# RWKV-7 recurrence and a cosine-gated MLP on one core: first loads in another order, back substitution over more segments, k, v, r behind x^T, sine passes and weight pieces in smaller works

## The chip, the core and the metric

The kernel runs on one core of a Trainium2 chip. A core has five engines with an instruction stream each: PE (TensorE, matrix products; its weight loads are listed as PEld), DVE (VectorE), ACT (ScalarE), POOL (GpSimd) and SP (SyncE, here only an issuer of DMAs). Each stream is worked off in order, and an engine waits on semaphores for the others. The metric is the device time of one execution in microseconds, the median of several runs.

## The reference

Two blocks follow each other. The first is a recurrence with a 40 x 40 state for each of 4 batches and 8 heads over 768 tokens, the second an MLP on its output, turned into 3072 tokens of 320 channels, with 2048 hidden units and g = h cos(h). The weights come as 64-bit floats.

```python
for t in range(S):
    y[:, :, t] = np.einsum('bhd,bhde->bhe', rt, state)
    Sa = np.einsum('bhde,bhe->bhd', state, at)
    state_decay = state * wt[:, :, None, :] - np.einsum('bhd,bhe->bhde', Sa, bt)
    state = state_decay + np.einsum('bhd,bhe->bhde', vt, kt)
...
h = x @ w_in
g = h * np.cos(h)
return g @ w_out
```

## The kernel before

**Chunks.** The recurrence runs over 24 chunks of 32 tokens (`NCH`, variable `c`), the four batches together on 128 partitions. A chunk is written as a list of *segments*, each a group of matmuls on PE and the work that takes their results out of PSUM:

- `t`, `q`, `x`, `s`, `z` (`ch_t` to `ch_z`, tiles `sT`, `qps`, `x0ps`, `sps`, `dps`) are the chain of the chunk itself. `z` renews the state `qz` and makes the output `yt`; the next `t` reads `qz`, so two chunks follow each other strictly.
- `v`, `k`, `g` (`p2_v`, `p2_k`, `p2_g`, tiles `vT`, `kT`, `gram`) prepare the next chunk from k, v and r.
- `p1` prepares chunks two at a time, some chunks ahead, from w, a and b: `p1_w` (tile `wT`; scans into `wb`, L311), `p1_a` twice (tile `wn`; reciprocal L327 and product `aT` L329), `p1_b` (tile `bT`) and `p1_n` (tile `nps`, product `nt`). Below these are w, a, a', b and n. In the main loop they are the list `extra`.

**Back substitution.** For every four chunks DVE inverts triangular 32 x 32 systems: `inv_start` transposes `nt` into `u` (L373), 31 times `inv_step` multiplies and subtracts (L381, L385; sizes rise from 31 to 256 elements per partition and fall again), `inv_end` transposes the result into `rt` (L389), which `s` of the four chunks reads. These 33 works stand in the list `inv_steps`, and the main loop puts some of them behind each step.

**Weights.** Each of 36 weight pieces comes as 64-bit words by a DMA from POOL's queue (`fetch`, three buffers `words`) and is turned into single precision in three works, `exponent`, `mantissa`, `product` (L197 to L219), on DVE and ACT. They stand in `w_steps`.

**The MLP** runs over 12 groups of two chunks (`g`) and four slices of the hidden units (`j`), in *pieces*: `first_a` and `first_b` (tile `ph`), then twice `second` (tile `po`) for the slice before. `first_b` also emits the sine passes: ACT adds a rounding constant (L614), DVE takes the fraction of the turns (L616), ACT takes the absolute value and the sine (L618, L619), DVE multiplies (L623). The products also free the PSUM of `ph`.

**x^T.** `tokens` sends `yt` to DRAM (`xd`) and, one step later, back as `xT`, both by SP's queue. The loads of k, v, r and w, a, b go by the same queue.

**The order** is written out by hand: `step` emits a work, then what `later` has put off by so many steps, then works of `inv_steps` and `w_steps`. The main loop emits the segments of a chunk, and after each the pieces that are due: eight per chunk, by a lag `START` of 2.4 chunks. So which engine does what in which order is fixed at build time, and an instruction waits for everything ahead of it on its engine. PSUM has two buffers (`at`) for all segments, two (`ps_h`) for `ph`, two (`ps_o`) for `po`.

## Time and profile before

| | us |
|---|---|
| median of 3 runs | 976.82 |
| lowest, highest | 975.35, 978.05 |
| the profiled execution | 975.64 |
| its span in the trace | 973.6 |
| PE, DVE, ACT, POOL busy | 782.4, 535.9, 355.3, 185.9 |

The profile page slices the span into 40 equal parts; each digit is a busy share in tenths, PEclk the clock that TensorE was granted. It shows a start of some ten slices in which DVE is full and PE is not, then a stretch in which PE is nearly full but for a dip about every sixth slice, and an end that PE fills alone.

```profile
PE   3605546686998997998888999888899887999987
DVE  4498887689426279335479324587335573233222
PEclk9555556787999997999997999999999998999999
```

The rows of the views that carry numbers stand in the prediction.

### The profile page before, as it was taken

To read this page: it belongs to the slowest core of one execution; us is meant where nothing else is said; L and a number is where in the kernel's file an instruction comes from. 1 tells how busy PE (TensorE), PEld (TensorE's weight loads), DVE (VectorE), ACT (ScalarE), POOL (GpSimd) and SP (SyncE) were. 2 spreads that over 40 slices of the span, in tenths; PEclk is the share of its full clock that TensorE was granted. 3 is DMA by queue.
4 is the path that set the end of the run, shared out by engine and by line. 5 is a ranking of instruction groups with operands and counts; after the bars stand their busy time and mean duration, and the time that the engine had idled before them with its cause. 6 is when DMAs were issued, how large, how long until landed. Compare 5 with 4: busy or idle time off the path is not lost.

```text
span 973.6 us, 36928 instructions
## 1 busy us (share of the span) xinstructions
PE 782.4 (80%) x16472; PEld 602.9 (62%) x16472; DVE 535.9 (55%) x1178; ACT 355.3 (36%) x671; POOL 185.9 (19%) x372
## 2 busy tenths in 40 slices
PE   3605546686998997998888999888899887999987
PEld 2504445465776675777666677666677665777765
DVE  4498887689426279335479324587335573233222
ACT  0103525441352432443432433422434332444333
POOL 4303342202123012023102112102202202111000
PEclk9555556787999997999997999999999998999999
DMA  6512637221321311312212213213211201200000
GB/s 95 94 29 84 155 87 157 63 52 20 70 42 38 57 37 30 65 38 48 50 35 45 48 38 55 56 22 55 45 32 37 51 3 36 44 25 17 23 23 13
DMA packets 181470, 49.06 MB, mean 50 GB/s; under 512 B 159040, under 2 KB 179008, under 8 KB 181312
## 3 DMA queue, kind: packets, MB, share of 16 engines
q1 hardware_dynamic: 174016, 35.56, 19.7%
q0 software_dynamic: 2944, 10.49, 3.6%
q8 instruction: 129, 2.11, 0.9%
q10 hardware_dynamic: 4352, 0.66, 0.4%
q14 instruction: 29, 0.24, 0.1%
HBM read 38.80 MB, written 7.86 MB: 48 GB/s over the span
## 4 chain that ended last, share of the span: by engine, by line
PE 49%; DVE 23%; ACT 10%; issue 6%; SPq 5%; DMA 4%; POOL 2%; POOLq 0%; ACTq 0%; DVEq 0%
PE ph L101 21%; PE po L101 13%; SPq L149 5%; DVE inv_tmp L381 4%; DVE inv L385 4%; ACT turns L614 2%; DVE wb L311 2%; PE qps L101 2%; PE gram L101 2%; DVE turns L616 2%; ACT turns L619 2%; ACT turns L618 2%; DMA xT<-xd 2%; PE sT L464 2%; PE dps L101 2%
## 5 line engine op out<-in xcount | busy, mean ns | idle before, releaser
L101 PE MATMUL po<-w_out_sb,gT 128*128 128x320 f32 x768 | 237.1, 455 | 1.0 <-issue 1.0
L101 PE MATMUL ph<-xT,w_in_sb 128*128 128x256 f32 x768 | 203.3, 412 | 22.6 <-DMA xT<-xd 14.3
L616 DVE SCALAR_TENSOR_TENSOR turns<-turns,ph 128x512 f32<-128x512 f32 x96 | 61.7, 684 | 259.3 <-ACT turns L614 259.3
L101 PEld LDWEIGHTS ph<-xT,w_in_sb 128*128 128x128 f32 x768 | 149.6, 204 | 48.3 <-issue 24.1
L101 PEld LDWEIGHTS po<-w_out_sb,gT 128*128 128x128 f32 x768 | 144.1, 197 | 56.7 <-issue 9.2
L614 ACT ACTIVATE turns<-ph,rnd 128x512 f32<-128x512 f32 x96 | 60.8, 684 | 150.3 <-PE ph L101 150.3
L554 POOL TENSOR_TENSOR qz<-qz,wc 128x160 f32<-128x160 f32 x92 | 41.4, 466 | 332.2 <-DVE qz L553 331.6
L623 DVE TENSOR_TENSOR gT<-ph,turns 128x512 f32<-128x512 f32 x96 | 63.1, 684 | 23.6 <-ACT turns L619 23.6
L385 DVE TENSOR_TENSOR inv<-inv,inv_tmp 128x31 f32<-128x31 f32 (+15 forms) x186 | 68.6, 369 | 6.4
L381 DVE TENSOR_TENSOR inv_tmp<-u,inv 128x31 f32<-128x31 f32 (+15 forms) x186 | 68.3, 367 | 5.1
L619 ACT ACTIVATE turns<-turns,half_pi 128x512 f32<-128x512 f32 x96 | 69.3, 722 | 3.1
L618 ACT ACTIVATE turns<-turns 128x512 f32<-128x512 f32 x96 | 59.7, 622 | 10.4 <-DVE turns L616 10.4
L101 PE MATMUL ph<-xT,w_in_tail 64*128 64x256 f32 x384 | 55.1, 406 | 0.0
L327 DVE RECIPROCAL rw<-wn 128x320 f32<-128x320 f32 x24 | 51.5, 2145 | 2.1 <-PE wn L270 2.1
L468 ACT COPY s<-sT 128x512 f32<-128x512 f32 x46 | 24.7, 588 | 58.5 <-PE sT L464 58.5
L200 ACT ACTIVATE expo<-expo,to_bits 128x256 int32<-128x256 int32 (+1 forms) x36 | 19.2, 533 | 72.7 <-DVE expo L197 72.7
L101 PEld LDWEIGHTS ph<-xT,w_in_tail 64*128 64x128 f32 x384 | 33.5, 188 | 18.8 <-issue 15.8
L522 ACT COPY sm<-sps 128x160 f32<-128x160 f32 x48 | 14.0, 291 | 77.8 <-DVE sm L526 43.4
L270 PE MATMUL wT<-ident,nat_w 128*128 128x128 f32 x88 | 14.6, 315 | 34.2 <-DVE x L505 23.7
L313 POOL COPY wc<-wb 128x16 f32<-128x16 f32 x24 | 5.4, 225 | 186.0 <-DVE wb L311 186.0
L101 PE MATMUL dps<-vvm,kn 32*64 32x72 f32 x1536 | 27.3, 255 | 16.8 <-ACT vvm L456 8.4
L101 PE MATMUL gram<-aT,kT 40*32 40x32 f32 x1536 | 19.2, 211 | 26.8 <-DVE wb L311 23.1
(104 smaller groups left out, 1107.7 us busy)
## 6 DMA issues: line engine op xcount, KB each, us to landing
words<-in_moe_w_out_dram POOLq DMA_DIRECT2D x16, 320.0 KB, 3.7
words<-in_moe_w_in_dram POOLq DMA_DIRECT2D x16, 256.0 KB, 3.6
nat_k<-in_k_dram SPq DMA_DIRECT2D x96, 40.0 KB
nat_v<-in_v_dram SPq DMA_DIRECT2D x96, 40.0 KB
nat_r<-in_r_dram SPq DMA_DIRECT2D x96, 40.0 KB
xd<-yt SPq DMA_DIRECT2D x48, 80.0 KB
out_dram<-ot SPq DMA_DIRECT2D x24, 160.0 KB
nat_w<-in_w_dram SPq DMA_DIRECT2D x88, 40.0 KB
```

Source lines behind the costliest of these rows:

```text
L101: nc.tensor.matmul(o, lhsT=lhsT, rhs=rhs, start=start, stop=stop, skip_group_check=True)
L149: via.dma_start(nat[n, c][blk[i], :, :D], src[n][i, :, c * C : (c + 1) * C, :].rearrange("h t d -> t h d"),)
L327: nc.vector.reciprocal(rw, unpad(ps[:, 0].rearrange("p (h d) -> p h d", h=H)))
L381: nc.vector.tensor_tensor(tmp, u[:, :j, j : j + 1].to_broadcast([P, j, C - j]), x[:, j : j + 1, j:].to_broadcast([P, j, C - j]), ALU.mult,)
L385: nc.vector.tensor_tensor(x[:, :j, j:], x[:, :j, j:], tmp, ALU.subtract)
L468: nc.scalar.copy(G["s"][:, 4 * i : 4 * i + 4].rearrange("p i e -> p (i e)"), ps[:, i])
L554: nc.gpsimd.tensor_tensor(z, z, wc.rearrange("p (f m b) -> p f m b", f=2, m=2)[:, :, :, bb] .unsqueeze(3).to_broadcast([P, 2, 2, D]), ALU. ...
L614: nc.scalar.activation(n, u, ACTF.Identity, bias=rnd, scale=1.0)
L616: nc.vector.scalar_tensor_tensor(n, n, -ROUND, u, ALU.add, ALU.subtract)
L618: nc.scalar.activation(n, n, ACTF.Abs)
L619: nc.scalar.activation(n, n, ACTF.Sin, bias=half_pi, scale=-2.0 * math.pi)
L623: nc.vector.tensor_tensor(gT[:, 2 * e : 2 * e + 2].rearrange("p f t -> p (f t)"), us[e], ns[e], ALU.mult)
```

## The change

It has five parts.

1. **First loads** (`load` calls): w before a, a of chunks 2 and 3 from SP's queue in place of ACT's, then b, w, a, b, k, v, r in the order of first use. The loads of w, a, b for two chunks are interleaved tensor by tensor.
2. **Back substitution**: where a chunk's number leaves 2 on division by four, b and n stand right behind `t` and `q`, and v, k, g behind them; so its works start in that chunk's middle and go on with one per step (before: from the end of that chunk, two per step). Where it leaves 3, w stands behind `t`, and k behind `x`. Works that are left are emitted only ahead of the first `s` that needs `rt`. The buffer `inv` is cleared with the later half of `nt`.
3. **k, v, r** of the next chunk: three separate works, three to five steps after `p2_kn` (before: one work, two steps after), so that SP issues x^T first.
4. **Sine passes**: `first_b` emits absolute value and sine for its first half only; the second half and the products follow one and two steps later, at the latest with the next `first_a`.
5. **Weight pieces**: the mantissa of a piece is emitted between exponent and product of the piece before; `mant` gets a second buffer.

```diff
@@ -151,13 +151,15 @@
                     src[n][i, :, c * C : (c + 1) * C, :].rearrange("h t d -> t h d"),
                 )
 
-    for c in range(4):
+    for c in range(2):
+        load(c, "w")
         load(c, "a", nc.scalar)
-    for c in (0, 2):
-        for n in "wb":
-            load(c, n)
-            load(c + 1, n)
-    load(0, "kvr")
+    for names in ("b", "wab"):
+        for n in names:
+            for c in range(2):
+                load(c if names == "b" else c + 2, n)
+    for n in "kvr":
+        load(0, n)
 
 
 
@@ -201,7 +203,7 @@
 
         def mantissa():
             lo, hi = t["words"][:, :, 0], t["words"][:, :, 1]
-            t["mant"] = sb1.tile([P, DM], I32, tag="mant", name="mant")[:n, :wid]
+            t["mant"] = sb2.tile([P, DM], I32, tag="mant", name="mant")[:n, :wid]
             frac = t["mant"].bitcast(F32)
             nc.vector.tensor_scalar(t["mant"], hi, 0xFFFFF, None, ALU.bitwise_and)
             nc.vector.scalar_tensor_tensor(
@@ -218,7 +220,7 @@
             )
             nc.vector.tensor_tensor(dst, t["mant"].bitcast(F32), expo.bitcast(F32), ALU.mult)
 
-        return fetch, [exponent, mantissa, product]
+        return fetch, exponent, mantissa, product
 
     def weights():
 
@@ -235,7 +237,8 @@
                 for rows, part in src:
                     nc.gpsimd.dma_start(dst[rows], part)
 
-            work.append((fetch, [lambda: nc.scalar.mul(dst, dst, by)]))
+            none = lambda: None
+            work.append((fetch, none, none, lambda: nc.scalar.mul(dst, dst, by)))
 
         for j in range(NF // 4):
             cs = slice(4 * j * P, 4 * (j + 1) * P)
@@ -274,7 +277,7 @@
     flat = lambda t: t.rearrange("p q t -> p (q t)")
     b4 = lambda t: t.rearrange("p (q t) -> p q t", t=C)
     unpad = lambda t: t[:, :, :D]
-    G = {}
+    G = {"rest": []}
 
     waiting = []
 
@@ -362,7 +365,7 @@
                 su.rearrange("p j t -> p (j t)").unsqueeze(1).to_broadcast([P, 2, HH * C]),
                 ALU.mult,
             )
-        if c % 4 == 0:
+        if c % 4 == 2:
             G["inv"] = sb1.tile([P, C * C], F32, tag="inv", name="inv")
             nc.gpsimd.memset(G["inv"], 0.0)
             nc.gpsimd.memset(G["inv"][:, :: C + 1], -1.0)
@@ -409,7 +412,8 @@
         nc.gpsimd.tensor_tensor(unpad(kn_b[c % 2]), nat["k", c], G["rw", c], ALU.mult)
         nc.gpsimd.tensor_copy(vvm[c % 2][:, :, C : C + D], nat["v", c])
         if c + 1 < NCH:
-            later(2, lambda: load(c + 1, "kvr"))
+            for i, n in enumerate("kvr"):
+                later(3 + i if c else 1, lambda n=n: load(c + 1, n))
 
     def p2_v(c):
         ps = at("vT")
@@ -589,7 +593,7 @@
 
 
     def first_a(g, j):
-        products()
+        rest(3)
         G["ph"] = [ps_h.tile([P, 2, 2 * P], F32, tag="h", name="ph") for _ in range(2)]
         G["gT", j] = sb2.tile([P, 4, 2 * P], F32, tag="gT", name="gT")
         first_full(g, j, 0)
@@ -614,22 +618,25 @@
             nc.scalar.activation(n, u, ACTF.Identity, bias=rnd, scale=1.0)
         for u, n in zip(us, ns):
             nc.vector.scalar_tensor_tensor(n, n, -ROUND, u, ALU.add, ALU.subtract)
-        for n in ns:
+        gT = G["gT", j]
+
+        def cosine(n):
             nc.scalar.activation(n, n, ACTF.Abs)
             nc.scalar.activation(n, n, ACTF.Sin, bias=half_pi, scale=-2.0 * math.pi)
-        gT = G["gT", j]
 
         def product(e):
             nc.vector.tensor_tensor(
                 gT[:, 2 * e : 2 * e + 2].rearrange("p f t -> p (f t)"), us[e], ns[e], ALU.mult
             )
 
-        G["products"] = [lambda e=e: product(e) for e in range(2)]
-        later(1, products)
-
-    def products():
-        for work in G.pop("products", ()):
-            work()
+        cosine(ns[0])
+        G["rest"] = [lambda: cosine(ns[1]), lambda: product(0), lambda: product(1)]
+        later(1, lambda: rest(2))
+        later(2, lambda: rest(1))
+
+    def rest(n):
+        for _ in range(min(n, len(G["rest"]))):
+            G["rest"].pop(0)()
 
     def second(g, j, i):
 
@@ -670,8 +677,8 @@
         def last_a():
             p1_a(c + 1)
             if c >= 2 and c + 3 < NCH:
-                for i in range(2):
-                    later(2 + i, lambda i=i: load(c + 2 + i, "wab"))
+                for i in range(6):
+                    later(2 + i, lambda i=i: load(c + 2 + i % 2, "wab"[i // 2]))
 
         return [lambda: p1_w(c), lambda: p1_a(c), last_a, lambda: p1_b(c), lambda: p1_n(c)]
 
@@ -712,8 +719,12 @@
             work()
 
         w_ends = []
-        for n, (_, parts) in enumerate(w_work):
-            w_steps.extend(parts)
+        w_steps.append(w_work[0][2])
+        for n, (_, exponent, _, product) in enumerate(w_work):
+            w_steps.append(exponent)
+            if n + 1 < len(w_work):
+                w_steps.append(w_work[n + 1][2])
+            w_steps.append(product)
             if n + 3 < len(w_work):
                 w_steps.append(w_work[n + 3][0])
             w_ends.append(len(w_steps))
@@ -734,18 +745,21 @@
                 extra = (p1(q0)[3:], p1(q0 + 2)[:3], p1(q0 + 2)[3:])[c % 4]
             if c == 0:
                 segs = [x, v, extra[0], s, k, extra[1], z, g, *extra[2:]]
-            elif len(extra) == 3:
+            elif c % 4 == 1 and extra:
                 segs = [t, v, q, k, x, extra[0], s, g, z, *extra[1:]]
-            elif len(extra) == 2:
+            elif c % 4 == 2 and extra:
+                segs = [t, extra[0], q, extra[1], x, v, s, k, z, g]
+            elif c % 4 == 3 and extra:
+                segs = [t, extra[0], q, v, x, k, s, g, z, *extra[1:]]
+            elif c % 4 == 0 and extra:
                 segs = [t, v, q, k, x, g, s, extra[0], z, extra[1]]
             else:
                 segs = [t, v, q, k, x, g, s, z]
             n = len(segs)
-            if c % 4 == 0:
-                while inv_steps:
+            fill = (1, 4 if c < 2 else 3)
+            for i, seg in enumerate(segs):
+                while seg is s and ("rt", c) not in G:
                     inv_steps.pop(0)()
-            fill = (1 + (c % 4 == 3), 4 if c < 2 else 3)
-            for i, seg in enumerate(segs):
                 step(seg, *fill)
                 due = (c + (i + 1) / n - START) * 8
                 while done < min(due, len(pieces)) and 2 * pieces[done][0] + 2 <= c:
```

The following rows are instructions in the order of their engine's stream: line, operation, result and operands, elements, and how often in a row. The first are DVE's in chunk 7 before, around the scans of `wT` (L311); L381 and L385 are one step of the back substitution.

```order
L505 COPY x_6808<-x0ps 128x288
L623 TENSOR_TENSOR gT<-ph,turns 128x512 x2
L381 TENSOR_TENSOR inv_tmp<-u,inv 128x252
L385 TENSOR_TENSOR inv<-inv,inv_tmp 128x18x14
...
L381 TENSOR_TENSOR inv_tmp<-u,inv 128x255
L385 TENSOR_TENSOR inv<-inv,inv_tmp 128x15x17
L308 MEMSET wT 128x32
L311 SCALAR_TENSOR_TENSOR wb<-wT,w_188 128x512
L311 SCALAR_TENSOR_TENSOR wb<-wT,w_190 128x512
L381 TENSOR_TENSOR inv_tmp<-u,inv 128x252
L385 TENSOR_TENSOR inv<-inv,inv_tmp 128x14x18
```

The same place of the changed kernel, whose lines 311, 314, 384, 388, 620, 628 and 509 are the former 308, 311, 381, 385, 616, 623 and 505:

```order
L384 TENSOR_TENSOR inv_tmp<-u,inv 128x240
L388 TENSOR_TENSOR inv<-inv,inv_tmp 128x20x12
L311 MEMSET wT 128x32
L314 SCALAR_TENSOR_TENSOR wb<-wT,w_188 128x512
L314 SCALAR_TENSOR_TENSOR wb<-wT,w_190 128x512
L384 TENSOR_TENSOR inv_tmp<-u,inv 128x247
L388 TENSOR_TENSOR inv<-inv,inv_tmp 128x19x13
...
L620 SCALAR_TENSOR_TENSOR turns<-turns,ph 128x512 x2
L384 TENSOR_TENSOR inv_tmp<-u,inv 128x255
L388 TENSOR_TENSOR inv<-inv,inv_tmp 128x15x17
L509 COPY x_6831<-x0ps 128x288
L628 TENSOR_TENSOR gT<-ph,turns 128x512
```

Ahead of the scans stand twelve of the 31 steps where there were seventeen, and this chunk's first sine pass (L620) and the copy of `x` (L509) now come behind the scans.

SP's stream at the turn from chunk 19 to 20 before (`xd` and `xT` carry the tokens, the others are loads for a later chunk):

```order
L574 DMA xd<-yt 40x4x128 x2
L149 DMA nat_k<-in_k_dram 32x8x40 x4
L149 DMA nat_v<-in_v_dram 32x8x40 x4
L149 DMA nat_r<-in_r_dram 32x8x40 x4
L584 DMA xT<-xd 128x2x128
L586 DMA xT<-xd 64x128 x2
```

and in the changed kernel:

```order
L578 DMA xd<-yt 40x4x128 x2
L588 DMA xT<-xd 128x2x128
L590 DMA xT<-xd 64x128 x2
L149 DMA nat_k<-in_k_dram 32x8x40 x4
L149 DMA nat_v<-in_v_dram 32x8x40 x4
L149 DMA nat_r<-in_r_dram 32x8x40 x4
```

The twelve loads have moved behind the three DMAs that bring x^T back.

DVE's first weight pieces in chunk 0 before (L197 is the exponent, L206 and L207 the mantissa, L216 and L219 the product):

```order
L197 TENSOR_SCALAR expo<-words 128x256
L206 TENSOR_SCALAR mant<-words 128x256
L207 SCALAR_TENSOR_TENSOR mant<-words,mant 128x256
L216 SCALAR_TENSOR_TENSOR expo<-words,expo 128x256
L219 TENSOR_TENSOR w_in_sb<-mant,expo 128x256
```

and in the changed kernel, where the lines are 199, 208, 209, 218 and 221:

```order
L208 TENSOR_SCALAR mant<-words 128x256
L209 SCALAR_TENSOR_TENSOR mant<-words,mant 128x256
L199 TENSOR_SCALAR expo<-words 128x256
L208 TENSOR_SCALAR mant<-words 128x256
L209 SCALAR_TENSOR_TENSOR mant<-words,mant 128x256
L218 SCALAR_TENSOR_TENSOR expo<-words,expo 128x256
L221 TENSOR_TENSOR w_in_sb<-mant,expo 128x256
```

A mantissa (for the piece after) now stands between a piece's exponent and its product.

## The prediction

> **What bounds the kernel now.** I first read the page's head, then cut the trace at every `sT` group on PE (the first matmuls of a chunk, from chunk 1 on), because the 24 chunks do not have one limit.
>
> ```profile
> span 973.6 us, 36928 instructions
> PE 782.4 (80%) x16472; PEld 602.9 (62%) x16472; DVE 535.9 (55%) x1178; ACT 355.3 (36%) x671; POOL 185.9 (19%) x372
> ```
>
> The table of windows has, per chunk, the length, the busy time of PE, PEld, DVE, ACT and POOL (instructions in brackets), the granted PE clock, the DMA share and GB/s. In order these are chunks 0, 2, 3, 6, 7, 9, 11, 14, 15, 18, 19, 20 and 21.
>
> ```profile
> 75.20:108.40 33.20, 14.15 (x477) 11.65 (x477) 28.50 (x62) 11.75 (x26) 12.71 (x24) 0.50 0.38 99
> 143.70:194.80 51.10, 32.83 (x724) 25.27 (x725) 36.22 (x87) 26.16 (x49) 14.92 (x27) 0.71 0.45 105
> 194.80:244.00 49.20, 35.53 (x637) 27.39 (x636) 44.04 (x108) 16.60 (x32) 7.08 (x14) 0.82 0.17 37
> 311.70:345.90 34.20, 31.71 (x748) 24.00 (x749) 15.56 (x31) 14.12 (x26) 6.17 (x12) 0.95 0.32 61
> 345.90:387.40 41.50, 33.54 (x638) 26.14 (x637) 34.56 (x85) 12.52 (x24) 6.53 (x13) 0.88 0.15 29
> 421.60:453.40 31.80, 30.11 (x637) 23.57 (x636) 12.43 (x25) 12.52 (x24) 6.15 (x13) 1.00 0.18 34
> 487.70:530.10 42.40, 34.84 (x638) 26.81 (x637) 35.10 (x88) 12.52 (x24) 6.64 (x13) 0.84 0.17 32
> 596.00:630.00 34.00, 30.12 (x749) 23.16 (x750) 14.45 (x28) 14.11 (x26) 6.20 (x12) 1.00 0.32 61
> 630.00:671.20 41.20, 32.89 (x637) 25.77 (x636) 35.54 (x88) 12.52 (x24) 6.55 (x13) 0.92 0.17 31
> 737.20:772.20 35.00, 31.74 (x748) 24.00 (x749) 15.92 (x32) 14.11 (x26) 6.25 (x12) 0.95 0.15 34
> 772.20:804.50 32.30, 29.18 (x614) 22.20 (x613) 25.07 (x70) 11.99 (x22) 2.26 (x5) 0.94 0.11 21
> 804.50:841.40 36.90, 30.24 (x614) 22.63 (x613) 13.74 (x33) 12.61 (x24) 5.52 (x11) 0.91 0.16 34
> 841.40:868.90 27.50, 27.34 (x613) 20.84 (x612) 8.90 (x22) 12.43 (x23) 5.39 (x10) 1.00 0.17 33
> ```
>
> Chunk 9 (remainder 1 by four) is PE's: 30.1 us of matmul in 31.8 us, DVE 12.4 us. Chunks 7, 11 and 15 (remainder 3) have the same segments and matmul counts, yet take 41.2 to 42.4 us: DVE is busy for 35 us there, PE's clock falls to 0.84 to 0.92, and PE's own busy time swells to 33 to 35 us. Up to chunk 3, DVE sets the pace too (28.5 of 33.2 us in chunk 0). So the prize is in chunks 3, 7, 11, 15 and 19, and in the start; chunk 21 (27.3 of 27.5 us) shows a chunk in which nothing is left.
>
> PE's timeline in chunk 7 says which waits end last; the bracket is idle time and what ended it:
>
> ```profile
> 360.84 2.32 PE L101 MATMUL po<-w_out_sb,gT 128*128 128x320 f32 x8
> 368.40 0.83 PE L101 MATMUL gram<-aT,kT 40*32 40x32 f32 x60 [4.43 <-DVE wb L311]
> 375.63 0.81 PE L101 MATMUL dps<-vvm,kn 32*64 32x72 f32 x52 [1.95 <-ACT vvm L456]
> 387.35 1.06 PE L464 MATMUL sT<-ident,qz 128*128 128x128 f32 x8 [1.58 <-DVE aT L329]
> ```
>
> All three follow DVE: `gram` needs the PSUM buffer that the scans of `wT` (L311) release. DVE's and POOL's own timelines there:
>
> ```profile
> 345.53 0.21 DVE L385 TENSOR_TENSOR inv<-inv,inv_tmp 128x31 f32<-128x31 f32 x1
> 351.64 0.39 DVE L385 TENSOR_TENSOR inv<-inv,inv_tmp 128x220 f32<-128x220 f32 x1
> 365.91 2.34 DVE L311 TENSOR_TENSOR_SCAN wb<-wT,w 128x512 f32<-128x512 f32 x2
> 380.49 1.20 DVE L381 TENSOR_TENSOR inv_tmp<-u,inv 128x87 f32<-128x87 f32 x1
> 380.29 1.29 POOL L565 TENSOR_TENSOR yt<-yt,wb 128x512 f32<-128x512 f32 x1
> ```
>
> `wT` was on PE by 361.0 us, but its scans start at 365.9 us, behind back-substitution steps.
>
> **The change, part by part.**
>
> *Back substitution.* The page's groups give its price:
>
> ```profile
> L385 DVE TENSOR_TENSOR inv<-inv,inv_tmp 128x31 f32<-128x31 f32 (+15 forms) x186 | 68.6, 369 | 6.4
> L381 DVE TENSOR_TENSOR inv_tmp<-u,inv 128x31 f32<-128x31 f32 (+15 forms) x186 | 68.3, 367 | 5.1
> ```
>
> (68.6 + 68.3) / 6 = 22.8 us for each of the six inversions, plus two transposes; nothing of it is removed. It moves: `b` and `n` go to the front of remainder-2 chunks, so 11 of its 33 works (the transpose and ten steps) issue there, 19 in the remainder-3 chunk, three in the next, one per step. From the rows, the ten small steps take 351.64 + 0.39 - 345.53 + 0.2, about 6.7 us; the last two, short as the first, about 0.9 us. So 15.2 us stay in chunks 7, 11, 15, and DVE has 12.4 + 15.2 = 27.6 us there instead of 35. The segment `w` also moves up, behind `t`; ahead of its scans then stand two steps of this chunk, not the backlog. The wait for the scans becomes that of `v`: between `w` and `v` PE has one piece and `q`, about 3 us, and copies plus scans take 0.3 + 2.34 us and a little queueing: I take 0.7 us. Beside it I leave 1.0 us at `dps` (of 1.95) and 0.4 us at the next `sT`, which needs a 2.1 us reciprocal on a busier DVE than in chunk 9. That gives 31.8 + 0.7 + 1.0 + 0.4 = 33.9, taken as 34 us: bounds are 31.8 (chunk 9) and 41.2 (unchanged). Gain: 41.5 + 42.4 + 41.2 - 3 x 34 = **23.1 us**. Chunk 3 has 44.0 us of DVE work now, 3.5 us of it the last weight pieces and the rest of the inversion; without 7 to 8 us that move out and the stalls, 37.5 us: **11.7 us** (bounds 5 and 15).
>
> The works that arrive in remainder-2 chunks (8.8 us with the transpose) lie beside PE's 30 us: DVE has 15 of 34 us busy. What is late next there is `g`, now right behind `z`, waiting for `z`'s PSUM as `n` did, some 0.7 us longer because a step stands ahead of the adds. With the waits for x^T gone (below) I take 33.5 us: 34.2 + 34.3 + 34.0 - 3 x 33.5 = **2.0 us** (chunk 10 is 34.3 us, between the two shown) and 35.0 - 33.5 = **1.5 us** for chunk 18. If that cover fails, each of these four loses what a remainder-3 chunk loses now (a rival).
> Chunk 19 issues 16 steps instead of 32; 28.3 us, near chunk 21: **4.0 us**.
>
> *x^T before k, v, r on SP's queue.* Chunk 19 to 20, SP first, then PE, and PE at chunk 22, where no such loads are in between:
>
> ```profile
> 806.42 0.70 SPq L574 DMA_DIRECT2D xd<-yt  x2
> 813.07 0.45 SPq L584 DMA_DIRECT2D xT<-xd  x1
> 815.28 2.04 PE L101 MATMUL ph<-xT,w_in_sb 128*128 128x256 f32 x4 [6.60 <-DMA xT<-xd]
> ...
> 874.68 1.97 PE L101 MATMUL ph<-xT,w_in_sb 128*128 128x256 f32 x8 [1.69 <-DMA xT<-xd]
> ```
>
> The 12 loads hold x^T back from 807.1 to 813.1 us; the trip through DRAM still needs xd to land, so I keep 2.0 us of wait as at chunk 22 and 0.3 us of lower clock: 27.5 + 2.3 = 29.8 us, **7.1 us**. In other even chunks this wait was at most 1 us and is in the 33.5. What the loads lose, xd's landing and three issues, some 4 us of lead, hides behind the chunk: in the program their first reader, the copy into `vp`, stands behind this chunk's `g`, and `v` of the chunk after needs it. If that fails, `v` waits.
>
> *First loads.* Rows of ACT, PE and POOL:
>
> ```profile
> 6.20 4.99 ACTq L149 DMA_DIRECT2D w_in_sb<-in_a_dram  x8
> 11.28 1.28 ACT L307 ACT_TABLE_LOAD   x1 [11.28 <-DMA w_in_sb<-in_a_dram]
> 7.89 1.09 PE L270 MATMUL wT<-ident,nat_w 128*128 128x128 f32 x4 [1.74 <-DMA nat_b<-in_b_dram]
> 33.87 0.45 POOL L403 COPY vp<-nat_v 128x320 f32<-128x320 f32 x1
> ```
>
> ACT issues eight loads that nobody needs yet and copies from `wT` at 12.57 us, though PE is done at 9.0 us. Without them the table load falls into the wait for `wT`: 12.57 - 9.1, **3.4 us**. The eight DMAs go to SP, some 5 us of issue, ahead of k, v, r, which then land near 30 us; POOL needs v at 33.87 - 3.4 = 30.5 us, so the cover is thin (if it fails, 1 to 2 us). Bounds 1 and 4.
>
> *Weight pieces.* DVE's waits from 75 to 250 us (total, count, longest) and the page's line of the fetch:
>
> ```profile
> DVE w_in_sb L219 <- ACT mant L210: 7.4, 13, 2.8
> DVE w_out_sb L219 <- ACT mant L210: 4.4, 14, 0.6
> words<-in_moe_w_out_dram POOLq DMA_DIRECT2D x16, 320.0 KB, 3.7
> ```
>
> With the next piece's mantissa ahead of the product, these 11.8 us go. But a piece's words are then needed half a piece earlier, so part may return as a wait for the fetch (3.7 us to land, a piece takes about 3 us with what lies between). I take **5 us** in chunks 0 and 1 and nothing in chunk 2, where DVE gains seven back-substitution us against the rest. Bounds -8 and 12.
>
> *Sine passes.* ACT's second pair (0.62 + 0.72 us) and the products come one or two steps later; the PSUM that they free is needed again four pieces later, so zero, bounds -4 and 3.
>
> **Two rules weighed.** "SBUF — State Buffer" of the Trainium skill (the single rule) has a VectorE instruction with two SBUF inputs block against a GpSimd one that reads SBUF; the 1.20 us for 87 elements at 380.49, beside POOL's `yt`, agrees. By it, spread steps meet POOL in two chunks instead of one: about 1 us more of DVE per inversion, and the time would be 4 us higher were DVE the bound in both.
> "TensorE: Matmul & The Clock Gate" of the Trainium skill (Part 1) has the clock halve after an idle window of about 3.4 us. The next rows, chunk 12, differ: a 1.48 us wait, and `po` takes 3.88 us instead of 2.32. By the page's rule the shorter gaps that I leave cost no clock and the four remainder-2 chunks would gain about 1.5 us each (913 in all, inside the forecast).
>
> ```profile
> 558.65 1.36 PE L101 MATMUL nps<-aT,bT 40*32 40x32 f32 x128 [1.48 <-DVE yt L560]
> 559.94 3.88 PE L101 MATMUL po<-w_out_sb,gT 128*128 128x320 f32 x8
> ```
>
> By the row, remainder-0 chunks keep that dip, and remainder-2 chunks may keep it with `g` in the place of `n`; the sum goes by the row.
>
> **The sum.** 23.1 + 11.7 + 2.0 + 1.5 + 4.0 + 7.1 + 3.4 + 5 = 57.8 us. The profiled execution took 975.64 us (2.0 us around its span): 917.8. The median of the runs is 976.82, 1.2 higher: **919 us**.
>
> **Rivals.**
> - *DVE still rules remainder 3* (27.6 us in order, idle while it waits for ACT): half the gain in chunks 7, 11, 15 and 3 goes, 17.4 us: 936. For: DVE idles ahead of the turns it must wait for. Against: 6 us of slack in 34.
> - *The words come late*: a third of the 22 or so pieces of chunks 0 and 1 wait 1.6 us, 13 us lost instead of 5 won: 937.
> - *Better*: remainder 3 reaches chunk 9's 31.8 us (6.6 us), chunk 2 loses its stalls with chunk 3 (7 us): 905.
> - *The wait only moves*: `v` waits for the scans as long as `gram` did, and chunks 3, 7, 11, 15 gain nothing: 919 + 34.8 = 954. It needs DVE to lag by 4 us at `w`.
> - *Slower*: a back-substitution step costs by standing ahead of PE's releases in DVE's one queue, not by its length. Then remainder-3 chunks keep their 42 us and chunks 2, 6, 10, 14 and 18 become the like, 8 us more each: 976.8 + 40 - 3.4 - 7.1 - 5 = 1001. It decides if DVE lags by over 3 us at `z` in chunk 6, where it has 19 us free.
>
> **Chances.** Forecast (897 to 930) 0.55, DVE rules 0.18, words 0.07, better 0.12, only moves 0.04, slower 0.04. A range of 897 to 947 leaves out the last two. About 0.3% is what measurements of this kernel can tell from no change. Faster by more: 0.95; within: 0.01; slower: 0.04.
>
> **What would show it.** Chunks 7, 11, 15 at 34 us with PE's clock near 1.00, DVE busy about 28 us there and 24 us in chunks 6, 10, 14; no 4.43 us wait at `gram`, under 1 us at `v`; `ph` in chunk 20 waiting about 2 us for x^T, whose issue follows xd's; the first scans near 9.5 us; no DVE wait for `mant`, and few for `words`. Wrong would be a wait over 3 us at `v` or `g`, or chunk 6 over 36 us.

## The result and the profile after

| | before | after |
| --- | --- | --- |
| median of the runs, us | 976.73 (975.35 to 978.05) | 940.34 (938.98 to 943.47) |
| ratio, with its 95% interval | 1 | 0.9632 [0.9603, 0.9661] |
| span of the profiled execution, us | 973.6 | 937.8 |
| PE busy, us | 782.4 | 775.1 |

The change makes the kernel 36.4 us faster; the forecast was 57.8. From the page after: the span, the busy times, the packets that bring instructions (queue, kind, packets, MB, share of 16 engines), and who holds the chain that ends last.

```profile
span 937.8 us, 36893 instructions
PE 775.1 (83%) x16472; PEld 598.6 (64%) x16472; DVE 536.5 (57%) x1178; ACT 357.0 (38%) x671; POOL 189.3 (20%) x372
q8 instruction: 130, 2.13, 0.9%
PE 64%; DVE 18%; issue 6%; DMA 5%; ACT 4%; SPq 2%; POOL 1%; POOLq 0%; ACTq 0%; DVEq 0%
```

The table of windows after, for chunks 3, 6, 7, 10, 11, 14, 18 and 20; the columns are those of the prediction.

```profile
197.70:241.00 43.30, 33.22 (x637) 25.71 (x636) 35.29 (x84) 17.01 (x33) 9.03 (x17) 0.88 0.17 42
309.00:348.10 39.10, 33.98 (x749) 25.83 (x750) 21.06 (x46) 14.42 (x26) 7.45 (x14) 0.87 0.29 54
348.10:380.30 32.20, 30.28 (x638) 23.58 (x637) 25.52 (x60) 12.56 (x24) 6.80 (x13) 1.00 0.17 36
443.60:484.20 40.60, 33.43 (x749) 25.38 (x750) 23.05 (x51) 14.43 (x26) 7.41 (x14) 0.87 0.30 57
484.20:515.90 31.70, 30.13 (x637) 23.56 (x635) 23.66 (x55) 12.56 (x24) 6.87 (x13) 1.00 0.14 29
580.10:614.10 34.00, 31.10 (x749) 24.11 (x750) 21.16 (x46) 14.31 (x26) 7.51 (x14) 0.95 0.33 62
710.30:747.70 37.40, 32.61 (x749) 25.07 (x750) 20.73 (x45) 14.43 (x26) 7.50 (x14) 0.91 0.14 30
775.10:805.40 30.30, 28.12 (x614) 20.91 (x614) 16.18 (x41) 12.94 (x25) 6.01 (x12) 1.00 0.19 42
```

Chunks 7 and 11 came down from 41.5 and 42.4 us to PE's own 30 us of work plus little. But chunks 6, 10 and 18, which were to win 0.7 to 1.5 us each, lost 4.9, 6.3 and 2.4 us, with PE's clock at 0.87 to 0.91. Chunk 14 has the same segments and lost nothing. VectorE is not full in any of them (21 to 23 us). So PE's own timeline in chunk 10 comes next: idle time before a group and its releaser stand in brackets.

```profile
454.31 1.29 PE L101 MATMUL nps<-aT,bT 40*32 40x32 f32 x128
456.34 0.77 PE L101 MATMUL x0ps<-qz,aT 40*32 40x72 f32 x51
459.25 0.35 PE L101 MATMUL x0ps<-qz,aT 40*32 40x72 f32 x13 [2.14 <-issue]
459.53 4.11 PE L101 MATMUL po<-w_out_sb,gT 128*128 128x320 f32 x8
...
476.31 0.71 PE L101 MATMUL gram<-aT,kT 40*32 40x32 f32 x62 [2.10 <-DVE yt L564]
479.84 0.31 PE L101 MATMUL gram<-rT,vT 40*32 40x32 f32 x3 [2.15 <-issue]
480.08 4.27 PE L101 MATMUL po<-w_out_sb,gT 128*128 128x320 f32 x8
```

PE stops in the middle of `x0ps`, after 51 of 64 passes (a pass is one MATMUL instruction of PE; each has its own weight load on PEld), and in the middle of `gram`, for 2.14 and 2.15 us. The releaser is "issue": it waits for nothing that the profile shows, and its operands were there, since the other passes of the same group had run. Behind both stops `po` takes over 4 us instead of 2.32. The 2.10 us wait of `gram` for `yt` is the one that the prediction expected there. Chunk 14 has that wait as well but no stop, and its second slow `po` comes all the same, so that one belongs to the wait for `yt`:

```profile
608.82 0.86 PE L101 MATMUL gram<-aT,kT 40*32 40x32 f32 x62 [2.11 <-DVE yt L564]
...
610.18 4.08 PE L101 MATMUL po<-w_out_sb,gT 128*128 128x320 f32 x8
```

Against chunk 14, chunks 6, 10 and 18 are 5.1, 6.6 and 3.4 us longer. Their stops, with what `po` behind the one in `x0ps` takes over 2.42 us, make up 4.3, 6.0 and 3.4 us of it. The trace lists when each packet of queue q8, which brings instructions, started and landed; worked out from it, all in us:

```
chunk   PE stops in   from      to        packet started  landed   landing to PE's restart
6       x0ps          322.21    324.33    321.37          322.84   1.49
10      x0ps          457.11    459.25    456.37          457.84   1.41
10      gram          477.69    479.84    477.19          478.59   1.25
18      x0ps          723.06    724.81    722.42          723.36   1.45
```

Each stop begins 0.50 to 0.84 us after a packet of 16 KB has started and ends 1.25 to 1.5 us after it has landed. PE and PEld run 16472 + 16472 = 32,944 instructions in 130 packets, about 253 each, so a packet is taken to hold 256. No two of the 130 packets start within 3.3 us. `n` and `x` are 128 passes and 128 weight loads each, two packets' worth in some 3 us of work (454.3 to 457.2 us without the stop). In the kernel before, a piece stood behind `x`; its PE rows in chunk 6:

```profile
323.20 0.88 PE L101 MATMUL x0ps<-qz,aT 40*32 40x72 f32 x64
324.01 2.42 PE L101 MATMUL po<-w_out_sb,gT 128*128 128x320 f32 x8
326.53 0.73 PE L101 MATMUL gram<-aT,kT 40*32 40x32 f32 x62
```

The new order has ten segments for eight pieces, none behind the fourth (`n`) and the ninth (`z`), so that `n` meets `x`, and `z` meets `g`.

### The profile page after: what moved, and what is told of

The parts are those of the page before. It is cut to its first block, busy times and chain, and to the rows that moved or that the text cites. A ratio compares the mean times of both kernels' runs of the same rounds, so it can differ in the third digit from the quotient of the medians.

```text
span 937.8 us, 36893 instructions
## 1 busy us (share of the span) xinstructions
PE 775.1 (83%) x16472; PEld 598.6 (64%) x16472; DVE 536.5 (57%) x1178; ACT 357.0 (38%) x671; POOL 189.3 (20%) x372
## 4 chain that ended last, share of the span: by engine, by line
PE 64%; DVE 18%; issue 6%; DMA 5%; ACT 4%; SPq 2%; POOL 1%; POOLq 0%; ACTq 0%; DVEq 0%
PE ph L101 24%; PE po L101 19%; PE x0ps L101 4%; DVE inv_tmp L384 3%; PE dps L101 3%; DVE inv L388 3%; DVE rw L330 2%; PE gram L101 2%; DVE turns L620 2%; SPq L149 2%; PE qps L101 2%; PE vT L273 2%; PE sT L468 2%; PE sps L101 2%; ACT turns L618 2%
## 5 line engine op out<-in xcount | busy, mean ns | idle before, releaser
L101 PE MATMUL po<-w_out_sb,gT 128*128 128x320 f32 x768 | 243.6, 465 | 0.0
L101 PE MATMUL ph<-xT,w_in_sb 128*128 128x256 f32 x768 | 193.2, 396 | 13.9 <-DVE gT L628 6.2
L620 DVE SCALAR_TENSOR_TENSOR turns<-turns,ph 128x512 f32<-128x512 f32 x96 | 61.7, 684 | 219.8 <-ACT turns L618 219.8
L101 PEld LDWEIGHTS po<-w_out_sb,gT 128*128 128x128 f32 x768 | 148.7, 203 | 58.5 <-issue 13.3
L101 PEld LDWEIGHTS ph<-xT,w_in_sb 128*128 128x128 f32 x768 | 143.1, 195 | 36.0 <-issue 13.3
L628 DVE TENSOR_TENSOR gT<-ph,turns 128x512 f32<-128x512 f32 x96 | 65.0, 684 | 18.3 <-ACT turns L625 18.0
L384 DVE TENSOR_TENSOR inv_tmp<-u,inv 128x31 f32<-128x31 f32 (+15 forms) x186 | 71.8, 386 | 4.2 <-POOL inv L371 0.4
L388 DVE TENSOR_TENSOR inv<-inv,inv_tmp 128x31 f32<-128x31 f32 (+15 forms) x186 | 69.5, 374 | 6.4
L273 PE MATMUL wT<-ident,nat_w 128*128 128x128 f32 x88 | 14.4, 315 | 32.2 <-DVE x L509 25.3
L557 DVE TENSOR_TENSOR qz<-dps,qz 128x160 f32<-128x160 f32 x92 | 29.1, 317 | 19.1 <-PE dps L101 19.0
L530 DVE TENSOR_TENSOR sm<-sps,su 128x128 f32<-128x128 f32 x48 | 14.0, 291 | 45.1 <-ACT sm L526 45.1
L273 PE MATMUL bT<-ident,bn 128*128 128x128 f32 x96 | 18.6, 327 | 25.3 <-ACT bT L343 18.7
L468 PE MATMUL sT<-ident,qz 128*128 128x128 f32 x184 | 26.5, 288 | 11.4 <-DVE aT L332 11.4
```

The source lines that it names most:

```text
L101: nc.tensor.matmul(o, lhsT=lhsT, rhs=rhs, start=start, stop=stop, skip_group_check=True)
L273: nc.tensor.transpose(ps[:, i * P : (i + 1) * P], x[:, 2 * i : 2 * i + 2].rearrange("p e d -> p (e d)"), ident)
L384: nc.vector.tensor_tensor(tmp, u[:, :j, j : j + 1].to_broadcast([P, j, C - j]), x[:, j : j + 1, j:].to_broadcast([P, j, C - j]), ALU.mult,)
L388: nc.vector.tensor_tensor(x[:, :j, j:], x[:, :j, j:], tmp, ALU.subtract)
L468: nc.tensor.transpose(ps[:, i // 4, (i % 4) * P : (i % 4 + 1) * P], qz[:, i // 2, i % 2, C : C + P], ident)
L620: nc.vector.scalar_tensor_tensor(n, n, -ROUND, u, ALU.add, ALU.subtract)
```

## The experiments

Three theories of the loss in chunks 6, 10 and 18 stand against each other: A, PE's instructions do not arrive in time where groups of small matmuls follow each other; B, the back substitution spread into these chunks holds them up; C, the loads of w, a, b issued there do. All ratios are to the kernel before, run on the same chip in the same session. In the expectations, "standing" is PE standing idle.

**e1, e2, e3: a piece between the small groups.** One number in the due time of the pieces, for chunks 2, 6, 10, 14 and 18 alone:

```diff
-                due = (c + (i + 1) / n - START) * 8
+                due = (c + (i + 1) / n - START) * 8 + 0.1 * (c % 4 == 2)              # e1
+                due = (c + (i + 1) / n - START) * 8 + 0.1 * (c % 4 == 2 and i == 3)   # e2
+                due = (c + (i + 1) / n - START) * 8 + 0.1 * (c % 4 == 2 and i == 8)   # e3
```

> The changed kernel with the due time of the pieces moved by 0.1 piece in chunks 2, 6, 10, 14, 18, so that a piece (po) now stands between n and x and between z and g there, and none between x and v or between g and the next t. Theory A (instruction fetch): TensorE gets its instructions in packets of 16 KB, 130 for about 33,250 instructions, no two of which start within 3.3 us; n and x back to back, and z and g, are 256 instructions each in 4 us, so TensorE stands inside them until a packet has come, and the clock falls behind that. Expected: no standing of over 0.5 us inside x0ps or gram in chunks 6, 10, 18, po behind them near 2.32 us in place of 4.1 to 4.6, chunks 6, 10 and 18 at 33.5 to 35.5 us in place of 39.1, 40.6 and 37.4, all in all 925 to 929 us. Theory B (the spread back substitution on VectorE holds up these chunks): chunks 6 and 10 stay over 38 us, 938 to 942 us. Theory C (loads of w, a, b in these chunks stand in the way): as B.

> The changed kernel with only the piece between n and x in chunks 2, 6, 10, 14, 18 (taken from between x and v); z and g stay back to back. Theory A: the standing inside x0ps (2.12, 2.14 and 1.74 us in chunks 6, 10, 18) goes, with the 1.8 to 2.3 us that the po behind it lost: about 4 us each in chunks 6, 10 and 18, 928 to 932 us; standing inside gram may stay. If the wait of gram for yt on VectorE (2.1 us, then po at 3.6 to 4.3 us) is what costs: 937 to 941 us. Theories B and C: 938 to 942 us.

> The changed kernel with only the piece between z and g in chunks 2, 6, 10, 14, 18 (taken from between g and the next t); n and x stay back to back. Theory A: the standing inside x0ps stays, as long as the packets fall at the same instructions; the wait of gram for yt goes under the piece, and the one standing of 2.15 us inside gram in chunk 10: 2 to 3 us in each of four chunks, 930 to 936 us. If the wait for yt is the whole loss: 926 to 930 us. Theories B and C: 938 to 942 us.

Measured: e1 921.97 us, ratio 0.9451 [0.9390, 0.9512]; e2 933.02 us, 0.9543 [0.9479, 0.9607]; e3 933.24 us, 0.9555 [0.9496, 0.9613]. Windows of chunks 6, 7 and 10 in e1:

```profile
308.70:338.90 30.20, 29.43 (x748) 22.86 (x748) 16.70 (x38) 13.92 (x25) 4.28 (x10) 1.00 0.35 64
338.90:373.20 34.30, 30.62 (x649) 23.56 (x638) 29.43 (x66) 12.83 (x25) 10.02 (x18) 1.00 0.18 39
439.60:472.40 32.80, 29.77 (x749) 23.09 (x749) 19.16 (x40) 13.93 (x25) 6.78 (x13) 1.00 0.34 64
```

PE's work is the same, and chunks 6 and 10 take 30.2 and 32.8 us instead of 39.1 and 40.6, at full clock. e1 alone does not exclude B, though: VectorE's work slid from chunk 6 (21.06 to 16.70 us) into chunk 7 (25.52 to 29.43 us), which rose from 32.2 to 34.3 us and pays part of the gain back. The clean comparison is e2, where VectorE keeps its work in chunk 6:

```profile
310.70:345.50 34.80, 31.98 (x748) 24.52 (x749) 21.10 (x46) 14.29 (x26) 7.42 (x14) 0.91 0.33 62
```

In e2 no stop in `x0ps` is left in chunks 6, 10 and 18; they shortened by 4.3, 3.9 and 3.5 us, and chunk 14 by nothing. So the piece behind `n` undoes the stop with the slow `po` behind it, while back substitution and loads stay in place: A stands, and B and C fall as the cause of the stops. What is left of B is some 0.6 us of the wait for `yt` (2.10 us, where `n` waited 1.48 us in chunk 12 before): one step stands ahead of the adds.

e1 gained more than A's numbers had it (925 to 929), because the wait of `gram` for `yt` now lies under the piece as well. But A had also expected no stop over 0.5 us, and chunk 10 of e1 keeps one in `gram`, although a piece stands ahead of it (e2 has one of 2.01 us there):

```profile
472.17 0.28 PE L101 MATMUL gram<-rT,vT 40*32 40x32 f32 x11 [2.24 <-issue]
```

In e3 `x0ps` still stops (1.55, 1.59 and 1.76 us), and the four chunks are at 31.8, 31.9, 30.1 and 33.9 us, with VectorE's work moved out as in e1. Each half alone brings about 7 us (e2 came out 1 us above its range), both 18. In chunks 6, 10, 14 and 18 the halves gain 11.6 and 23.4 us and both together some 27 us; what is lost again elsewhere differs, and why was not followed up.

**h1: the disputed cost by itself.** Small matmuls for which nothing can wait, behind the last output:

```diff
+        # indices shortened
+        for n in range(512):
+            mm(ps[...], w_in_sb[half[e], 0, ...], w_in_sb[half[e], 1, ...], n < 8)
+            if n >= 256 and n % 16 == 15:
+                mm(po, w_in_sb[:, 0, :P], w_in_sb[:, 1, :DM], True)
```

> The changed kernel with a probe behind the last output: 512 matmuls of 40x32 on resident weights that nothing waits for, and whose result is left; the first 256 back to back, the other 256 with a matmul of 128x320 after each 16. Every matmul here is two passes, so four instructions with its weight loads: the first 256 are 1024 instructions, four packets. By the durations of the small groups (64 passes in 0.88 us) they take 7 us at full clock. Theory A: they take 13 to 17 us, with standing of 1 to 2.5 us about once per packet, ended by nothing that the profile shows; the other 256 show no standing, or next to none. Rival (the standings in the kernel were waits that the profile does not see, for data or a buffer): no standing in the first 256 either, 7 to 8 us at full clock, or evenly slower at a lower one.

The timeline of h1, PE alone, and the windows of its two halves:

```profile
937.76 2.45 PE L101 MATMUL dense<-w_in_sb 40*32 40x32 f32 x243
941.97 1.53 PE L101 MATMUL dense<-w_in_sb 40*32 40x32 f32 x128 [1.76 <-issue]
945.44 1.54 PE L101 MATMUL dense<-w_in_sb 40*32 40x32 f32 x128 [1.94 <-issue]
948.91 0.73 PE L101 MATMUL dense<-w_in_sb 40*32 40x32 f32 x45 [1.94 <-issue]
949.58 1.43 PE L101 MATMUL wide<-w_in_sb 128*128 128x320 f32 x2
950.94 0.47 PE L101 MATMUL dense<-w_in_sb 40*32 40x32 f32 x32
```

```profile
937.76:949.58 11.82, 6.18 (x546) 5.77 (x545) 0.00 (x0) 0.43 (x1) 0.00 (x0) 0.64 0.10 31
949.58:977.40 27.82, 27.82 (x517) 12.96 (x512) 0.00 (x0) 0.00 (x0) 0.00 (x0) 0.50 0.01 3
```

PE stops after each 128 passes, that is 256 instructions, and restarts every 3.47 us. The packets of q8 started at 939.55, 943.02, 946.55 and 950.03 us; landing to restart was 1.54, 1.46 and 1.31 us, as in the kernel. There is nothing else to wait for, so the rival of hidden data waits falls. The first half took 11.8 us (13 to 17 were expected: by the 243 passes ahead of the first stop, some two packets were already there). The second half, with a wide matmul after each 16, never stops. It ran at half clock, where 68 instructions (16 small matmuls and a wide one) took 1.76 us, so 256 took about 6.6 us; whether it would stop at full clock, this run does not show.

**f1, f4: the spread back substitution and the loads of k, v, r.** f1 is the kernel before with the new segment order and the new places of the back substitution alone; f4 is the changed kernel with one edit undone:

```diff
-            for i, n in enumerate("kvr"):
-                later(3 + i if c else 1, lambda n=n: load(c + 1, n))
+            later(2, lambda: load(c + 1, "kvr"))
```

> The kernel before with the new segment order and the spread back substitution alone (first loads, loads of k, v, r and of w, a, b, sine passes and weight pieces as before). Theory of the prediction: this part alone takes chunks 7, 11, 15 from 41.2 to 42.4 us down to 32 to 34 us (25 to 29 us) and some 6 us off chunk 3; with the instruction fetch of theory A it also brings the standing inside x0ps in chunks 6 and 10 (chunks 6 and 10 at 38 to 41 us) and leaves chunks 19 and 20 at 32 and 37 us: 948 to 958 us. Rival: the short chunks 7, 11, 15 need the earlier loads of k, v, r too; then they stay over 36 us here, 960 us or more.

> The changed kernel with the loads of the next k, v, r as before (all three two steps after kn, ahead of x^T in SyncE's queue). Theory of the prediction: chunks 19 and 20 go back to about 32 and 37 us (from 27.4 and 30.3), the others stay: 949 to 954 us. Rival: with the new order of segments x^T is hidden in any case, 938 to 943 us.

f1: 960.33 us, 0.9859 [0.9782, 0.9937], with chunks 7, 11 and 15 at 33.1 us each, chunk 19 at 27.6 us, chunk 20 at 37.1 us, and stops in `x0ps` of 1.78, 1.84 and 1.74 us in chunks 6, 10 and 18. So this part alone makes the third chunk of each four short and brings the stops. The whole came out above the expectation because chunk 8 stays at 37.6 us, 2.69 us of it a stop inside `nps`. f4: 949.74 us, 0.9740 [0.9679, 0.9800], as expected in sum. The PE row for x^T in chunk 20, first after, then f4:

```profile
781.86 1.97 PE L101 MATMUL ph<-xT,w_in_sb 128*128 128x256 f32 x8 [2.18 <-DVE inv_tmp L384]
```

```profile
786.77 3.75 PE L101 MATMUL ph<-xT,w_in_sb 128*128 128x256 f32 x8 [6.84 <-DMA xT<-xd]
```

The first row names VectorE's `inv_tmp`, which `ph` does not read. SP's queue shows what it waited for:

```profile
779.62 0.38 SPq L588 DMA_DIRECT2D xT<-xd  x1
```

`ph` starts 2.24 us behind this issue; in f4 it starts 2.39 us behind the same issue (784.38 us), and in the kernel before 2.21 us (813.07 and 815.28 us). So the wait is still the trip of x^T. Chunk 20 goes back to 37.0 us in f4. Chunk 19 stays at 27.6 us, so its gain is the back substitution's, as the prediction had it; the expectation's 32 us for it was wrong.

**f2, g3: the sine passes.** Both have the two pairs of passes in one go again, in the changed kernel (f2) and in the best version below (g3):

```diff
-        cosine(ns[0])
-        G["rest"] = [lambda: cosine(ns[1]), lambda: product(0), lambda: product(1)]
-        later(1, lambda: rest(2))
-        later(2, lambda: rest(1))
+        for n in ns:
+            cosine(n)
+        G["products"] = [lambda e=e: product(e) for e in range(2)]
+        later(1, products)
```

> The changed kernel with the sine passes of a piece in one go as before (both cosines at once, both products one step later). Theory of the prediction: worth nothing, 938 to 942 us. Rival: the finer order lets copies on ScalarE that TensorE waits for pass between the passes, so without it 943 us or more.

> As g2_rem0_too, with the sine passes in one go as before. Undoing them in the changed kernel cost 10 us. Theory E: in the main it is ScalarE's queue (the copy of vvm stands behind sine passes, dps waits 1.4 us for it in each of chunks 7, 11, 15), so it costs 7 to 12 us here as well. Rival: half of it was the instruction fetch falling at a worse place (standing of 2.5 us inside nps in chunk 8), which is gone here, so 3 to 6 us.

f2: 950.42 us, 0.9734 [0.9679, 0.9788]; g3: 919.37 us, 0.9404 [0.9372, 0.9436], against 0.9302 without. Undoing the edit costs 10 us in both, so the prediction's zero was wrong. ACT in chunk 7, first f2, then after:

```profile
362.50 0.72 ACT L623 ACTIVATE turns<-turns,half_pi 128x512 f32<-128x512 f32 x1
363.13 0.61 ACT L622 ACTIVATE turns<-turns 128x512 f32<-128x512 f32 x1
363.77 0.72 ACT L623 ACTIVATE turns<-turns,half_pi 128x512 f32<-128x512 f32 x1
364.40 0.38 ACT L508 COPY x<-x0ps 128x288 f32<-128x288 f32 x1
```

```profile
361.09 0.72 ACT L625 ACTIVATE turns<-turns,half_pi 128x512 f32<-128x512 f32 x1
361.71 0.38 ACT L508 COPY x<-x0ps 128x288 f32<-128x288 f32 x1
```

In f2 the copy of `x` stands behind both cosines, after it stands between them. VectorE's half of that copy follows ACT's and is queued in order:

```profile
364.81 0.46 DVE L509 COPY x<-x0ps 128x288 f32<-128x288 f32 x1 [1.62 <-ACT x L508]
```

```profile
362.13 0.46 DVE L509 COPY x<-x0ps 128x288 f32<-128x288 f32 x1 [0.34 <-ACT x L508]
```

VectorE, the fullest engine beside PE there, stands 1.62 us instead of 0.34 with all its back substitution behind it, and `dps` then waits 1.09 us on PE for the copy of `vvm`. So it is ACT's queue, as theory E has it, but by the copy of `x`, not by the copy of `vvm`, which itself waits for VectorE. PE waits at `dps` for this copy in chunks 7, 11 and 15, 3.9 us in all in f2 and 4.0 in g3, and at `gram` for VectorE's scans in chunks 9, 13 and 17, 2.7 us in each run; in these chunks of the changed kernel and of g2 it waits at neither. That is 6.6 us of the 10 in both pairs. The rival, the packets, has a part too: chunk 8 has a stop of 2.46 us (f2) and 1.90 us (g3) inside `nps` where the other version has none. Chunks 2 and 5 are 2.0 to 2.4 us longer in both; the cause there was not looked for.

**e4, g1: the weight pieces.** Both have exponent, mantissa and product of a piece in a row again, with one buffer for `mant`; e4 is otherwise the changed kernel, g1 is e1.

```diff
-        w_steps.append(w_work[0][2])
-        for n, (_, exponent, _, product) in enumerate(w_work):
-            w_steps.append(exponent)
-            if n + 1 < len(w_work):
-                w_steps.append(w_work[n + 1][2])
-            w_steps.append(product)
+        for n, (_, parts) in enumerate(w_work):
+            w_steps.extend(parts)
```

> The changed kernel with the weight pieces as before (exponent, mantissa, product of one piece in a row, one buffer for the mantissa). Theory of the prediction: the finer order is worth 5 us in chunks 0 and 1, so 944 to 947 us. Rival: the mantissa of the next piece, asked for one step earlier, now waits for its words (9 us of such waits on VectorE between 106 and 241 us) and queues ahead of what TensorE waits for, so the new order is worth nothing or less: chunks 1 and 2 are shorter here than 37.1 and 53.8 us, 934 to 940 us.

> The changed kernel with the pieces moved in chunks 2, 6, 10, 14, 18 as in e1_both, and the weight pieces as before. If both gains add up: 2 to 3 us under e1_both's 922.0, so 918 to 921 us, with chunk 1 near 34 us. If the weight pieces' order only moved the same stall: 921 to 924 us.

e4: 938.25 us, 0.9604 [0.9554, 0.9655]; g1: 919.33 us, 0.9396 [0.9362, 0.9430], beside e1's 0.9451. The intervals overlap, so a loss by the new order isn't proved; a gain of 5 us shows in neither pair. Chunk 1 is 34.2 and 34.1 us with the old order against 37.1 and 36.9 with the new one. VectorE's waits from 75 to 250 us, after (total, times, longest):

```profile
DVE mant L208 <- DMA words<-in_moe_w_in_dram: 5.8, 5, 2.0
DVE mant L208 <- DMA words<-in_moe_w_out_dram: 4.0, 5, 1.9
```

The 11.8 us of waiting for ACT's `mant` are gone, as forecast, and 9.8 us of waiting for words have come in their place.

**f3: chunk 3.** `w` stands second in chunk 3, and `vT` waits there 6.17 us for its scans.

```diff
-            elif c % 4 == 1 and extra:
+            elif (c % 4 == 1 or c == 3) and extra:
```

> The changed kernel with chunk 3 alone in the old order of segments (t v q k x w s g z a a'), so that w no longer stands second there. Theory D: the shortfall of chunk 3 (43.3 us, 37.5 forecast) is the 6.17 us for which vT waits for the two scans of w on VectorE, which are queued behind weight pieces; without it chunk 3 takes 37 to 39 us, 934 to 936 us. Rival: VectorE's work (35.3 us busy in chunk 3) holds the chunk wherever w stands; the wait turns up at another place, chunk 3 stays at 42 to 46 us, 938 to 943 us.

f3: 937.21 us, 0.9603 [0.9547, 0.9658], the same as the change within the intervals; chunk 3 takes 43.8 us. PE's longest wait in chunk 3, after and in f3:

```profile
PE vT L273 <- DVE wb L314: 6.2, 1, 6.2
```

```profile
PE kT L273 <- ACT rT L425: 4.3, 1, 4.3
```

The wait only changed its place. Theory D falls; the rival, VectorE's 35 busy us of weight pieces and back substitution, fits, but which of the two would have to go wasn't tried.

**g2: the best version.** g1 with a piece between `z` and `n` in chunks 8, 12 and 16 too:

```diff
+                due = (c + (i + 1) / n - START) * 8 + 0.1 * (c % 4 == 2 or c % 4 == 0 and i == 8)
```

> As g1_both_old_weights, and in chunks 8, 12 and 16 the piece behind n stands between z and n instead. If it is the rule that two groups of small matmuls in a row cost a wait (nps for yt on VectorE 1.5 us) and a slow po behind it, each of these chunks gets 1.5 to 3 us shorter: 910 to 915 us. If the chunks are held by something else, the same as g1 within 1.5 us.

909.74 us, 0.9302 [0.9270, 0.9334], 30.6 us under the change. Chunk 10 in g2, PE:

```profile
441.08 2.42 PE L101 MATMUL po<-w_out_sb,gT 128*128 128x320 f32 x8
...
455.77 2.42 PE L101 MATMUL po<-w_out_sb,gT 128*128 128x320 f32 x8
458.13 0.72 PE L101 MATMUL gram<-aT,kT 40*32 40x32 f32 x61
```

`po` takes 2.42 us, `gram` no longer waits, and chunk 10 is 30.2 us long. Chunks 8, 12 and 16 went from g1's 32.3, 33.5 and 31.9 us to 30.4, 30.6 and 30.4 us.

## Why the prediction was right in sign and 21 us off

The forecast of 897 to 930 us was missed. The measured 940 us lie in the wider range up to 947 us, but that is luck in part. The upper part of that range stood for two rivals, at 936 and 937 us. The first, VectorE still ruling, did not happen: chunks 3, 7, 11 and 15 together gained 35.4 us, with 34.8 forecast. The second, late words, happened in part. The largest loss, 17.1 us against the forecast in chunks 6, 10, 14 and 18, came from a cause that no rival named. Gains that were not forecast, in chunks 7, 11 and 15 and in chunks without a term, made up for part of it.

Gains in us, from the chunks' lengths in the two profiled executions (973.6 - 937.8 = 35.8 in all):

| term | forecast | measured |
| --- | --- | --- |
| chunks 7, 11, 15 | 23.1 | 29.5 |
| chunk 3 | 11.7 | 5.9 |
| chunks 6, 10, 14 | 2.0 | -11.2 |
| chunk 18 | 1.5 | -2.4 |
| chunk 19 | 4.0 | 4.9 |
| chunk 20 | 7.1 | 6.6 |
| first loads and weight pieces (start, chunks 0, 1) | 8.4 | -0.2 |
| chunk 2 | 0 | -2.7 |
| all other chunks | 0 | 5.4 |
| sum | 57.8 | 35.8 |

- **Back substitution in chunks 7, 11, 15**: right in mechanism, shown by f1 (33.1 us each without the other parts; 34 forecast). The 4.43 us wait at `gram` is gone, the wait at `v` is 0.2 us, PE's clock is 1.00. VectorE is busy 23.7 to 25.8 us there, 28 forecast. f2, at 33.1 to 33.5 us, gives most of the further gain to the sine passes.
- **Chunks 6, 10, 14 and 18**: the step that failed. The prediction asked what is late next and named only `g` behind `z`; that wait came as forecast (2.10 us). It took PE's stream between its waits as fixed, and chunk 6 at 39.1 us is over the 36 us that it had named as a sign of being wrong. In place of a gain, the stops for instruction packets came in where `n` meets `x` and `z` meets `g` (h1, e1 to e3), some 14 of the 17.1 us. Where none fell, in chunk 14, the forecast's 33.5 us was 34.0. Those stops were in the trace of before as well, as idle time of PE "for issue" (1.85 us inside `gram` in chunk 3).
- **Sine passes**: "zero" was wrong, 10 us. The prediction looked at when PSUM comes free, not at the copy of `x` that stood behind both pairs in ACT's queue. By PE's new waits ACT's queue costs some 6.6 us of it; the rest is in part a stop for packets and in part open.
- **Weight pieces**: 5 us forecast, none measured. The wait that goes came back as a wait for the fetch, which the prediction named and put too low: the rival of the late words, in part.
- **x^T before k, v, r**: right; `ph` waits 2.18 us (2.0 forecast), and f4 brings a wait of 6.84 us back.
- **First loads**: the first scans start at 9.42 us (13.03 before; near 9.5 forecast), but chunk 1 starts only 1.6 us earlier. In e4 it starts at 106.2 us instead of 108.4, so about 2.2 of the 3.4 us last. This part was not tried alone.
- **Chunk 3**: half the gain. VectorE's work fell as forecast (44.0 to 35.3 us), but the chunk did not follow it down to 37.5 us: `v` waits 6.17 us for the scans, over the 3 us that the prediction had named as a sign of being wrong. That the place of `w` alone costs this was excluded by f3; what would free VectorE there stays open.
- **The shared SBUF port**: the rule of "SBUF — State Buffer" in the Trainium skill (the single rule) gave about 1 us more of VectorE per inversion. The page's groups after are (71.8 + 69.5) / 6 = 23.6 us against 22.8 us before, 0.7 us more by the sums 141.3 and 136.9, which agrees:

```profile
L384 DVE TENSOR_TENSOR inv_tmp<-u,inv 128x31 f32<-128x31 f32 (+15 forms) x186 | 71.8, 386 | 4.2 <-POOL inv L371 0.4
L388 DVE TENSOR_TENSOR inv<-inv,inv_tmp 128x31 f32<-128x31 f32 (+15 forms) x186 | 69.5, 374 | 6.4
```

## What to carry to other kernels

Before moving groups of small matmuls together, count their instructions, weight loads and passes included: 256 of them in under about 3.5 us outrun their own delivery here, and a wide matmul group moved between two small ones took most of these stops away with no added work on PE (one of 2.24 us stayed in e1). Idle time "for issue" inside a group of equal matmuls is a wait like any other and belongs in the sum. An edit that frees no engine, like sine passes split in two, was still worth 1% here, most of it because a copy that another engine waits for no longer stands behind both in the same queue.

## What the runs showed of the hardware

- **Instruction packets.** PE's 32,944 instructions came in about 130 packets of 16 KB, whose starts lie 3.31 us or more apart (3.21 us at the least in any run, in g3); PE restarted 1.25 to 1.54 us after a landing in all seven stops listed above. Where a stop falls depends on the execution too: h1 runs the same PE stream as the changed kernel up to its probe, yet stopped 2.12 us inside `nps` in chunk 8 (35.8 us, 32.3 after) and not inside `gram` in chunk 10 (37.6 us, 40.6 after). One chunk of one profile is good to some 3 us here.
- **The clock.** Behind stops of 2.1 us the granted clock fell to 0.61 (459.25 to 463.64 us), behind 1.55 us in e3's chunk 6 it stayed at 1.00. Yet `po` was slow behind a wait of 1.48 us in chunk 12 before, so the length of one stop does not decide it. "TensorE: Matmul & The Clock Gate" in the Trainium skill (Part 1) has it halve after an idle window of about 3.4 us and come back after as much busy time. The trace differs twice: shorter stops are enough, and in h1 the clock stayed at 0.50 for 27.82 us in which the profile, where the ends of matmuls are modelled, shows PE busy throughout. Why it did not come back there is open.
